# Two routed expert layers behind an attention: one stream of weight loads, and other places for rows, tables, scatters and steps

## The chip, the cores and the metric

One core of a Trainium2 chip runs the whole kernel. Its engines each work through their own list of instructions in a fixed order: TensorE (PE, matrix products and transposes), VectorE (DVE), ScalarE (ACT), GpSimd (POOL) and SyncE (SP, which here issues transfers); 16 DMA engines move the data. An instruction that has to wait holds up everything behind it on its engine. The metric is the time of one execution on the chip in microseconds (us), lower is better.

## The reference

Three stages follow each other. The first is an attention without softmax: for 8 batches and 8 heads, scores of 576 x 64 queries and keys, multiplied by a decaying causal mask, times the values. Its output is laid out as x, 4608 tokens of 512 columns.

The second is a mixture of experts (8 experts, 512 to 1024 to 512) in which each token goes to the one expert with the largest logit, weighted by its softmax value:

```python
logits = x @ w_gate
expert_idx = np.argmax(logits, axis=1)
...
for e in range(E):
    mask = expert_idx == e
    h = np.maximum(x[mask] @ w1[e], 0.0)
    out[mask] = gate_w[mask, None] * (h @ w2[e])
```

The third has the same shapes, but gives each expert exactly 576 tokens. All 4608 x 8 logits are gone through from the largest down, and a pair is taken if its token is free and its expert has room:

```python
for idx in np.argsort(-flat):
    tok, e = int(idx) // E, int(idx) % E
    if assigned[tok] >= 0 or counts[e] >= cap:
        continue
    assigned[tok] = e
    counts[e] += 1
```

and then each expert computes `np.maximum(x[mask] @ w1[e], 0.0) @ w2[e]` for its tokens.

## The kernel before, in words

Every matrix product is made of three products of halves: each float32 operand is split into a high and a low fp16 part, so that hi x hi, hi x lo and lo x hi give nearly float32. Weights arrive as float32 parts of 512 KB, eight per expert (four of w1, four of w2), in tiles named stage. ACT makes the high part (L384, w1h or w2h) and DVE the low part (L387, w1l or w2l). In `load_half` a half expert's loader issues three loads at once, converts a part at each of four later steps, and issues its fourth load after its first conversion. The next half's loads begin when its own loader is begun.

The order of work is written by hand around PE. `layer1` (L499) gives back control after every matrix product, `layer2` (L525; half tiles L521) too, and at numbered steps other work is put between them. Layer 1 of an expert has 192 such steps over its 640 rows, layer 2 has five tiles of 24. What is marked by `pe(...)` keeps its place in the written order; the rest is moved by the scheduler.

The first mixture (`moe1`): for each expert a list of its tokens is made (`cover` L537 to L539 on DVE, products L560 on PE, index arithmetic L563 to L569 on DVE), five gathers of 128 rows are issued on POOL (L418), and each row tile is squared and summed (L428 on DVE or L430 on ACT), scaled (L311 to L313, L443, L446, L447; POOL copies two columns, L448) and turned into columns (transposes on PE, or by DMA, L457). P0 holds the steps for expert 0's own list and its last two row tiles, N0, N1 and N6 those for the next expert's rows while experts 0, 1 to 5, and 6 run. L505 is the DVE operation that makes the low half of the hidden layer and so frees PE's result buffer. Tables for tokens beyond an expert's 640 rows (`overflow_tables`, DVE from L691 and one product, L769) are done a piece at a time in steps 38, 45, 52, ... of experts 2 and 3. Rows to fill gaps are scattered on POOL (L859) at steps of expert 6.

Layer 2 of experts 6 and 7 is put off: it runs while the second mixture makes its first choice.

The second mixture (`moe2`) runs eight phases. In each, `choose` finds the next expert and its tokens while an expert is computed: a threshold search (key L1268, comparisons L1272, counts on PE L1278 and L1287), the sums (L1310), the expert's number (es, L1318, read by SP, which then can load its weights), the table (V, L1334 or L1341; base L1345, copied at L1350), and the list (L537 to L539, L560). PACE and FIRST say how many PE columns go by between the steps, and GAP how many between tasks such as a conversion. The result rows are scattered to the output on POOL (L1446).

Of the kernel before, what the change touches and what calls it, by code (L numbers as in the profile page):

```python
# [9 lines left out]
F32 = mybir.dt.float32  # L10
# [17 lines left out]
SOON = 3  # L28
P0 = (3, 8, 52, 60)
N0 = (56, 76, 110, 130, 150, 170, 190)  # L30
N1 = (2, 32, 82, 102, 122, 142, 170)
# [310 lines left out]

def load_half(k, o, w, n, dve=0, spare=False, steps=True, behind=False):


    tc, nc = k.tc, k.nc
    if n == 1:
        o.wp = k.wp2 if k.wn % 2 else k.wp
        k.wn += 1
        o.w1h = o.wp.tile([128, 4, 1024], F16, name="w1h")  # L350
        o.w1l = o.wp.tile([128, 4, 1024], F16, name="w1l")
        h, l, shape, v = o.w1h, o.w1l, [128, 4, 256], w.rearrange("(c p) f -> p c f", p=128)
        at = lambda x, i: x[:, :, i * 256:(i + 1) * 256]
    else:
        if spare:
            o.w2h, o.w2l = (k.wp2.tile([128, 4, 1024], F16, name=x).rearrange("p c (a f) -> p (c a) f", a=2) for x in ("w1h", "w1l"))
        else:
            o.w2h = o.wp.tile([128, 8, 512], F16, name="w2h")
            o.w2l = o.wp.tile([128, 8, 512], F16, name="w2l")
        h, l, shape, v = o.w2h, o.w2l, [128, 2, 512], w.rearrange("(c p) f -> p c f", p=128)  # L360
        at = lambda x, i: x[:, 2 * i:2 * i + 2, :]

    def load(i):
        t = k.wp.tile(shape, F32, name="stage", bufs=3)
        d = nc.sync.dma_start(t, at(v, i))
        if behind:
            tc.keep_in_program_order(d)
        stages.append(t)

    stages = []  # L370
    for i in range(3):
        load(i)
    for i in range(4):
        yield
        t = stages[i]
        if i >= dve:
            if steps:
                pe(k, nc.scalar.activation(at(h, i), t, AF.Copy, scale=128.0))
            else:
                nc.scalar.activation(at(h, i), t, AF.Copy, scale=128.0)  # L380
            pe(k, nc.gpsimd.tensor_scalar(t, t, 128.0, 1.0, op0=OP.mult, op1=OP.mult))
            nc.gpsimd.tensor_tensor(at(l, i), t, at(h, i), op=OP.subtract)
        else:
            d = nc.scalar.activation(at(h, i), t, AF.Copy, scale=128.0)  # L384
            if steps:
                pe(k, d)
            d = nc.vector.scalar_tensor_tensor(at(l, i), t, 128.0, at(h, i), op0=OP.mult, op1=OP.subtract)  # L387
            if steps:
                pe(k, d)
        if i == 0:  # L390
            load(3)
    if n == 2:
        o.whole = True


def load_w(k, w1, w2, dve=0, spare=False):

    o = K()
    run(load_half(k, o, w1, 1, dve, steps=False))
    run(load_half(k, o, w2, 2, dve, spare, False))  # L400
    return o
# [21 lines left out]
def scale2(k, x, sc, q, dve=False, pin=False):  # L423

    nc = k.nc
    if dve:
        q = k.fp.tile([128, 512], mybir.dt.bfloat16, name="sq", bufs=1)
        nc.vector.scalar_tensor_tensor(q, x, 1.0, x, op0=OP.mult, op1=OP.mult, accum_out=sc[:, 0:1])  # L428
    else:
        d = nc.scalar.activation(q.bitcast(mybir.dt.bfloat16), x, AF.Square, accum_out=sc[:, 0:1])  # L430
        if pin:
            pe(k, d)
    normalizer(nc, sc[:, 0:1], sc[:, 1:2], sc[:, 2:3])


def normalise(k, xg, dve=False, to=None, pin=False):


    nc = k.nc
    h, sc = to or (k.fp.tile([128, 1024], F16, name="xhl", bufs=2), k.fp.tile([128, 6], F32, name="sc", bufs=12))  # L440
# [7 lines left out]
    nc.gpsimd.tensor_copy(sc[:, 4:6], xg[:, 512:514])  # L448
    return h, sc
# [152 lines left out]
def gate2(k, w, n):  # L602

    nc = k.nc
    pg = k.fps.tile([128, 8, 16], F32, name="tp")
    for i in range(4):
        t = k.fp.tile([128, 2, 8, 128], F16, name="w2T", bufs=2)
        for z, x in enumerate((w.w2h, w.w2l)):
            nc.sync.dma_start(t[:, z], x[:, 2 * i:2 * i + 2, :].rearrange("p f d -> p (f d)"), transpose=True)
# [41 lines left out]

def early(k, X, w1):


    nc = k.nc
    first = load_half(k, k.w[0], w1, 1, 2)
    next(first)
    yield
    yield
    for _ in range(4):  # L660
        next(first, None)
        yield
# [145 lines left out]
def moe1(k, X, X1, w1, w2):  # L808
# [6 lines left out]
    def prep(e):  # L815
# [47 lines left out]
    k.pin = True  # L863
    side = overflow_tables(k)
    x1, g, hs, ws, gates = None, {}, {}, {}, {}
    for e in range(8):
        w = ws[e] = k.w[e]
        steps = {}
        if e < 6:
            k.w[e + 1] = o = K()  # L870
            parts = [load_half(k, o, w1[e + 1], 1, 4), load_half(k, o, w2[e + 1], 2, 4)]
            if e == 0:
                parts[:0] = [load_half(k, w, w2[0], 2, 4)]
            if e == 5:
                k.w[7] = o = K()
                parts.append(load_half(k, o, w1[7], 1, 4))
        else:
            parts = [load_half(k, k.w[7], w2[7], 2, 4)] if e == 6 else []
        loader = chain(*parts)

        def load():
            next(loader, None)

        if e:
            load()
        for i in range(4, 190, 20) if e == 0 else range(13, 190, 30) if e == 5 else (16, 64, 112, 160):
            steps[i] = load
# [8 lines left out]
        if x1:  # L896
# [17 lines left out]
        if e == 6:  # L914
            for j in range(10 - LATE):
                steps[124 + 10 * j] = partial(put, k.fill, j, last)
        if e == 7:
# [15 lines left out]
        if e < 6:  # L933
            x1 = columns(e)
            for s in range(5):
                last = second(e, s, mixed(layer2(k, hs[e], w, s), {8: load, 18: load if e in (0, 5) and s < 2 else (lambda: None)}), x1)
    run(side)
# [512 lines left out]
def moe2(k, X1, w1, w2, out, rest):  # L1450
# [8 lines left out]
    def choices():  # L1459

        for ph in range(8):
            for t in choose(k, ph, lambda es: ev.setdefault(ph, nc.sync.value_load(es[0:1, 0:1], min_val=0, max_val=7)),
                            lambda ix: lx.setdefault(ph, ix)):
                yield (PACE if ph else FIRST)[t]

# [6 lines left out]

    def half(n, i):

        w = weights.setdefault(n, K())
        g = load_half(k, w, (None, w1, w2)[i][ds(ev[n], 1)].rearrange("o d f -> (o d) f"), i, 4)
        tasks.extend([(i == 1, lambda: next(g, None))] * 5)

# [21 lines left out]
    def prepare():  # L1500

        n = state.ph + 1
        if n == 0:
            if 0 in ev and 0 not in weights:
                half(0, 1)
        elif n in lx and n not in weights:
            half(n, 1)
            t = tasks[-5:]
            del tasks[-5:]
# [59 lines left out]
    turns[:] = [partial(turned, 0, s) for s in range(SOON, 5)]  # L1569
    half(0, 2)  # L1570
    for ph in range(8):
# [15 lines left out]
def program(tc, q, kk, v, wg1, w11, w12, wg2, w21, w22, consts, out, dbg=None):  # L1587
# [11 lines left out]
    select_setup(k)  # L1599
    k.w = {0: K()}  # L1600
    attention(k, q, kk, v, g1, X, early(k, X, w11[0]))
    open_ffn(k)
# [37 lines left out]
```

## Time and profile before

| | |
|---|---|
| median of 3 runs | 1130.11 us (1129.94 to 1133.36) |
| the profiled execution | 1129.93 us |
| its span, first to last instruction | 1128.1 us |
| mean granted TensorE clock | 0.978 |
| PE busy | 1061.4 us, 94% of the span |
| DVE busy | 668.7 us, 59% |
| ACT busy | 481.4 us, 43% |
| attention | 0 to 222 us |
| first mixture | 222 to 629 us; layer 2 of experts 6 and 7 until 697 us |
| second mixture | 697 to 1118 us; last scatter to 1128.1 us |

How to read the rows below: in a timeline a row has its start and its length in us, the engine, the line in the source, the operation with output<-input and shapes, and in brackets how long the engine had been idle before it and what released it. In a table of windows a row has the stretch in us, its length, the busy time and count of PE, its weight loads (PEld), DVE, ACT and POOL, then the granted clock of PE (1.00 is 2.4 GHz, 0.50 is 1.2 GHz), the share of the DMA engines and their GB/s. A row of waits has the waiting instruction, what it waited for, the sum over the run, how often, and the longest.

### The profile page before, as it was taken

To read this page: it belongs to the slowest core of one execution; us is meant where nothing else is said; L and a number is where in the kernel's file an instruction comes from. 1 tells how busy PE (TensorE), PEld (TensorE's weight loads), DVE (VectorE), ACT (ScalarE), POOL (GpSimd) and SP (SyncE) were. 2 spreads that over 40 slices of the span, in tenths; PEclk is the share of its full clock that TensorE was granted. 3 is DMA by queue.
4 is the path that set the end of the run, shared out by engine and by line. 5 is a ranking of instruction groups with operands and counts; after the bars stand their busy time and mean duration, and the time that the engine had idled before them with its cause. 6 is when DMAs were issued, how large, how long until landed. Compare 5 with 4: busy or idle time off the path is not lost. (4 is left out here: it accounts for less than half of the span.)

```text
span 1128.1 us, 25795 instructions
## 1 busy us (share of the span) xinstructions
PE 1061.4 (94%) x10279; PEld 682.9 (61%) x10279; DVE 668.7 (59%) x1662; ACT 481.4 (43%) x851; POOL 340.7 (30%) x589
## 2 busy tenths in 40 slices
PE   7999999789998999999989989899999999999996
PEld 5778877555646464746457534656565656567573
DVE  5787888775648455647553476747566646634140
ACT  5777766455545354536442124322233222224231
POOL 5766775041202020212040023323324141431101
PEclk9999999799999999999989999899999999999998
DMA  9999882349767677777966025538367392784211
GB/s 239 225 252 233 204 219 74 114 160 220 179 171 169 142 192 171 178 178 196 253 143 104 11 94 149 161 102 189 110 184 182 104 214 91 175 205 142 88 62 44
DMA packets 307520, 178.32 MB, mean 158 GB/s; under 512 B 241408, under 2 KB 274176, under 8 KB 307392
## 3 DMA queue, kind: packets, MB, share of 16 engines
q1 hardware_dynamic: 296928, 144.24, 52.6%
q0 software_dynamic: 10464, 32.34, 9.3%
q8 instruction: 84, 1.38, 0.5%
q14 instruction: 44, 0.36, 0.1%
HBM read 116.82 MB, written 31.28 MB: 131 GB/s over the span
## 5 line engine op out<-in xcount | busy, mean ns | idle before, releaser
L499 PE MATMUL ph<-xT,w1h 128*128 128x320 f16 (+4 forms) x2048 | 374.3, 299 | 11.9 <-DVE sc L312 4.9
L499 PEld LDWEIGHTS <-w1h 128*128 128x128 f16 x2048 | 200.3, 100 | 89.9 <-issue 24.3
L499 PE MATMUL ph<-xT,w1l 128*128 128x320 f16 (+4 forms) x1024 | 233.8, 299 | 0.0
L525 PE MATMUL py<-w2h,hh 128*128 128x512 f16 x536 | 203.2, 379 | 2.8 <-DVE key L1268 2.2
L525 PE MATMUL py<-w2l,hh 128*128 128x512 f16 x536 | 203.3, 379 | 0.0
L525 PE MATMUL py<-w2h,hl 128*128 128x512 f16 x536 | 203.2, 379 | 0.0
L525 PEld LDWEIGHTS <-hh 128*128 128x128 f16 x1072 | 103.1, 98 | 120.1 <-issue 4.9
L504 ACT ACTIVATE hh<-ph 128x576 f16<-128x576 f32 (+4 forms) x136 | 83.3, 613 | 181.7 <-PE ph L499 177.4
L505 DVE SCALAR_TENSOR_TENSOR hl<-ph,hh 128x576 f16<-128x576 f32 (+4 forms) x136 | 97.8, 719 | 69.0 <-ACT hh L504 67.9
L499 PEld LDWEIGHTS <-w1l 128*128 128x128 f16 x1024 | 100.9, 100 | 35.6 <-issue 3.3
L387 DVE SCALAR_TENSOR_TENSOR w1l<-stage,w1h 128x1024 f16<-128x1024 f32 x62 | 75.6, 1222 | 59.2 <-ACT w1h L384 58.1
L525 PEld LDWEIGHTS <-hl 128*128 128x128 f16 x536 | 52.4, 98 | 60.3
L387 DVE SCALAR_TENSOR_TENSOR w2l<-stage,w2h 128x1024 f16<-128x1024 f32 x64 | 78.3, 1224 | 12.0 <-ACT w2h L384 10.9
L384 ACT ACTIVATE w2h<-stage 128x1024 f16<-128x1024 f32 x64 | 66.9, 1048 | 8.7 <-DMA stage<-in_moe_w_dram 8.5
L430 ACT ACTIVATE x1r<-py 128x512 bf16<-128x512 f32 x40 | 23.8, 596 | 108.9 <-PE py L525 64.9
L384 ACT ACTIVATE w1h<-stage 128x1024 f16<-128x1024 f32 x62 | 64.2, 1046 | 8.7 <-DMA stage<-in_moe_w_dram 8.7
L1446 POOL DMA_INDIRECT out_dram<-x1r,ti x20 | 21.0, 1051 | 127.5 <-ACT x1r L1445 105.7
L1446 POOL DMA_INDIRECT out_dram<-w2T,ti x20 | 22.4, 1122 | 122.7 <-ACT w2T L1445 104.4
L418 POOL DMA_INDIRECT xg<-X1s,ix x40 | 44.7, 1116 | 44.2 <-DVE zf L1372 24.3
L583 POOL COPY x1r<-sc 128x1 f32<-128x1 f32 x37 | 8.5, 232 | 158.8 <-DMA X1s<-x1r 93.0
L187 DVE TENSOR_TENSOR sh<-pS,ct 128x1024 f16<-128x1024 f32 x36 | 43.9, 1220 | 17.3 <-PE pS L184 17.2
L147 POOL TENSOR_TENSOR vl<-vf,vh 128x512 f16<-128x512 f32 x36 | 41.7, 1159 | 36.1 <-ACT vh L146 28.9
(370 smaller groups left out, 1780.1 us busy)
## 6 DMA issues: line engine op xcount, KB each, us to landing
stage<-in_moe_w_dram SPq DMA_DIRECT2D x128, 512.0 KB, 4.1
Xs<-xr SPq DMA_DIRECT2D x36, 257.0 KB, 4.4
X1s<-x1r SPq DMA_DIRECT2D x33, 257.0 KB, 3.2
k<-in_k_dram SPq DMA_DIRECT2D x32, 256.0 KB, 4.3
q<-in_q_dram SPq DMA_DIRECT2D x32, 256.0 KB, 4.1
v<-in_v_dram SPq DMA_DIRECT2D x32, 256.0 KB, 4.4
k<-in_k_dram SPq DMA_DIRECT2D x8, 128.0 KB, 3.5
q<-in_q_dram SPq DMA_DIRECT2D x8, 128.0 KB, 3.7
```

What stands on the lines that cost most here:

```text
L147: nc.gpsimd.tensor_tensor(d.vl, d.vf, d.vh, op=OP.subtract)
L187: nc.vector.tensor_tensor(f(d.sh), f(pS), both, op=OP.mult)
L384: d = nc.scalar.activation(at(h, i), t, AF.Copy, scale=128.0)
L387: d = nc.vector.scalar_tensor_tensor(at(l, i), t, 128.0, at(h, i), op0=OP.mult, op1=OP.subtract)
L418: nc.gpsimd.indirect_dma_start(out=xg[:M], out_offset=None, in_=src, in_offset=bass.IndirectOffsetOnAxis(ap=gidx[:M], axis=0))
L430: d = nc.scalar.activation(q.bitcast(mybir.dt.bfloat16), x, AF.Square, accum_out=sc[:, 0:1])
L499: pe(k, nc.tensor.matmul(ph[:, z, :b], x[:, c, F], xT[:, y + c, a:a + b], start=i == 0, stop=i == 11))
L504: nc.scalar.activation(oh, src, AF.Relu)
L505: nc.vector.scalar_tensor_tensor(ol, src, 0.0, oh, op0=OP.max, op1=OP.subtract)
L525: pe(k, nc.tensor.matmul(py, x[:, f, S], y[:, f, :], start=i == 0, stop=i == 23))
L583: nc.gpsimd.tensor_copy(xr[:, 513:514], sc[:, 5:6])
L1446: nc.gpsimd.indirect_dma_start(out=out2 if tail else out, out_offset=bass.IndirectOffsetOnAxis(ap=ti, axis=0), in_=y, in_offset=None)
```

## The change

It has these parts, and what they compute is the same.

- `load_parts` takes the place of `load_half`. One stream holds all 64 parts of the first mixture; three loads are issued at the start, and after each conversion the load three parts on, over the borders of halves and experts. A number of parts that may be converted by the end of each expert caps it: (12, 20, 28, 36, 44, 56, 60, 60). In the second mixture each phase has such a stream over its w1 and w2.
- Expert 0's last two row tiles are normalised apart, at steps 40 and 60, and turned at 66 and 86 (before: normalised together, turned at 52 and 60); the next expert's rows come at 34, 70, 126, 146 and 168 and two in layer 2; xhl has three buffers instead of two. Conversions in expert 0 are 24 steps apart instead of 20.
- The overflow tables go through experts 1 to 4 at every 14th step instead of 2 and 3 at every 7th.
- The fill scatters are issued after the row tiles' last POOL copy (`issue_after`).
- In the first choice the list of PE's columns changes (base 3400 instead of 2000, list 1900 instead of 900), the key of phase 1 comes 5600 behind, and GAP is 3000 instead of 3800. Tasks stand in another order. The transposes of `gate2` keep their place on SP.
- The last phase computes its half tile first and a full tile last.

```diff
-P0 = (3, 8, 52, 60)
-N0 = (56, 76, 110, 130, 150, 170, 190)
+P0 = (3, 8, 40, 60, 66, 86)
+N0 = (34, 70, 126, 146, 168)
...
-FIRST = dict(key=2600, cnt=1700, any=1200, dig=800, sum=1900, base=2000, list=900)
-GAP = 3800
+FIRST = dict(key=2600, cnt=1700, any=1200, dig=800, sum=1900, base=3400, list=1900)
+AFTER_FIRST = 5600
+GAP = 3000
...
-def load_half(k, o, w, n, dve=0, spare=False, steps=True, behind=False):
...
-    for i in range(3):
-        load(i)
-    for i in range(4):
-        yield
...
-        if i == 0:
-            load(3)
+def load_parts(k, halves, steps=True):
...
+    for i in range(3):
+        load()
+    for m, ((o, w, n, dve, spare), i) in enumerate(parts):
+        yield
...
+        d = [nc.scalar.activation(h, t, AF.Copy, scale=128.0)]
...
+            d.append(nc.vector.scalar_tensor_tensor(l, t, 128.0, h, op0=OP.mult, op1=OP.subtract))
...
+        load()
...
-            normal = [normalise(k, x, True) for x in rows[e]]
+            normal = []
+            for x in rows[e]:
+                yield
+                normal.append(normalise(k, x, True, pin=True))
...
+    def fill(j, xr):
+        with k.tc.issue_after(k.copied.ins):
+            put(k.fill, j, xr)
...
+        due = (12, 20, 28, 36, 44, 56, 60, 60)[e]
         def load():
-            next(loader, None)
+            if k.parts < due:
+                k.parts += 1
+                next(k.loader, None)
...
-        if e in (2, 3):
-            for i in range(38, 192, 7):
+        if e in (1, 2, 3, 4):
+            for i in range(38, 192, 14):
...
-            tasks.extend([(True, partial(fetched, n))] + t[:2] + r[:2] + t[2:3] + r[2:4] + t[3:4] + r[4:] + t[4:])
-            half(n, 2)
+            tasks.extend(t[:1] + [(True, partial(fetched, n))] + t[1:3] + r[:2] + t[3:4] + r[2:4] + t[4:5] + r[4:] + t[5:])
...
-        for s in range(5):
+        for s in range(5) if ph < 7 else (4, 0, 1, 2, 3):
```

In expert 6 POOL's list had the scatters of fill rows (L859) around the gathers (L418) and the copies (L448) of expert 7's rows:

```order
L582 TENSOR_TENSOR x1r<-nm,sc 128x1
L850 COPY x1s<-x1r 128x1
L859 DMA X1s<-x1r,fill_7416 4736x514
L418 DMA xg<-Xs,ix 128x514 x5
L859 DMA X1s<-x1r,fill_7416 4736x514
L448 COPY sc<-xg 128x2 x4
L859 DMA X1s<-x1r,fill_7416 4736x514 x2
L448 COPY sc<-xg 128x2
L859 DMA X1s<-x1r,fill_7416 4736x514 x3
```

Now, with the lines of the changed source (L418 is L416 there, L859 is L861):

```order
L852 COPY x1s<-x1r 128x1
L582 TENSOR_TENSOR x1r<-nm,sc 128x1
L852 COPY x1s<-x1r 128x1
L416 DMA xg<-Xs,ix 128x514 x5
L448 COPY sc<-xg 128x2 x5
L861 DMA X1s<-x1r,fill_7281 4736x514 x7
```

All five gathers and all five copies now stand ahead of the seven scatters.

DVE's list at the first choice's lists, before. Two covers (L537 to L539, for two tables V) follow each other, then the index arithmetic:

```order
L1362 TENSOR_SCALAR few<-few 128x1
L537 TENSOR_SCALAR G<-iota_73,be 128x640
L538 TENSOR_SCALAR nV<-V_11162 128x44
L539 TENSOR_SCALAR G<-iota_73,be 128x640
L537 TENSOR_SCALAR G<-iota_73,be 128x640
L538 TENSOR_SCALAR nV<-V 128x44
L539 TENSOR_SCALAR G<-iota_73,be 128x640
L563 TENSOR_TENSOR lw<-slot_77,tp 128x5
```

The same place now (L312 to L314 are L311 to L313 of before, L1366 is L1362):

```order
L1366 TENSOR_SCALAR few<-few 128x1
L537 TENSOR_SCALAR G<-iota_73,be 128x640
L538 TENSOR_SCALAR nV<-V_11162 128x44
L539 TENSOR_SCALAR G<-iota_73,be 128x640
L387 SCALAR_TENSOR_TENSOR w1l<-stage,w1h 128x4x256
L312 TENSOR_SCALAR nm<-nm 128x1
L313 TENSOR_SCALAR nm<-nm 128x1
L314 TENSOR_SCALAR nm<-nm 128x1
L581 SCALAR_TENSOR_TENSOR x1r<-py,nm,x1r 128x512
L537 TENSOR_SCALAR G<-iota_73,be 128x640
L538 TENSOR_SCALAR nV<-V 128x44
L539 TENSOR_SCALAR G<-iota_73,be 128x640
```

A conversion of the phase's first part and the writing of a result row (L312 to L581) stand between the two covers. On PE the distance from the sums (L1310) to the base (L1345) goes from 10 products of L525 to 16, and from the base to the lists (L560) from 5 to 9.

DVE's list between the base and the second choice's lists (phase 1), before:

```order
L1350 COPY be<-tp 128x1
L1351 TENSOR_TENSOR be<-be,V 128x1
L1352 CAST V<-be 128x1
L505 SCALAR_TENSOR_TENSOR hl<-ph,hh 128x384
L387 SCALAR_TENSOR_TENSOR w2l<-stage,w2h 128x1024
L537 TENSOR_SCALAR G<-iota_73,be 128x640
L538 TENSOR_SCALAR nV<-V 128x44
L539 TENSOR_SCALAR G<-iota_73,be 128x640
```

and now (L1354 is L1350):

```order
L1354 COPY be<-tp 128x1
L1355 TENSOR_TENSOR be<-be,V 128x1
L1356 CAST V<-be 128x1
L505 SCALAR_TENSOR_TENSOR hl<-ph,hh 128x192
L537 TENSOR_SCALAR G<-iota_73,be 128x640
L538 TENSOR_SCALAR nV<-V 128x44
L539 TENSOR_SCALAR G<-iota_73,be 128x640
```

The conversion has left this place, and the hidden-layer operation ahead of the cover has half as many columns, since the choice now meets the second part of layer 1.

## Rows read from the trace of the kernel before

**Rows 1.** Page, engines' busy time; groups, last column idle before and releaser.

```profile
PE 1061.4 (94%) x10279; PEld 682.9 (61%) x10279; DVE 668.7 (59%) x1662; ACT 481.4 (43%) x851; POOL 340.7 (30%) x589
...
L384 ACT ACTIVATE w2h<-stage 128x1024 f16<-128x1024 f32 x64 | 66.9, 1048 | 8.7 <-DMA stage<-in_moe_w_dram 8.5
```

**Rows 2.** Waits of PE over the run: total us, times, longest us.

```profile
PE tp L560 <- DVE G L537: 5.6, 5, 2.8
PE tp L1345 <- DVE V L1334: 5.2, 4, 2.3
PE ph L499 <- DVE sc L312: 4.9, 2, 3.8
...
PE tp L1287 <- DVE r L1283: 2.9, 2, 2.1
...
PE tp L1278 <- DVE cmp L1272: 1.7, 1, 1.7
...
PE tp L1345 <- DVE V L1341: 1.1, 1, 1.1
```

**Rows 3.** Windows, layer 1 of experts 0, 1, 2, 6 with 7.

```profile
221.60:261.05 39.45, 33.09 (x225) 21.68 (x225) 28.59 (x89) 20.44 (x38) 13.70 (x23) 0.88 0.58 183
286.80:314.30 27.50, 27.50 (x244) 20.08 (x243) 20.35 (x55) 16.65 (x30) 7.13 (x14) 1.00 0.74 187
340.00:373.90 33.90, 30.56 (x245) 21.32 (x244) 27.12 (x98) 16.41 (x29) 8.27 (x14) 0.90 0.69 158
561.40:629.05 67.65, 62.55 (x647) 45.44 (x646) 30.34 (x87) 21.82 (x37) 13.58 (x19) 0.95 0.55 109
```

**Rows 4.** Windows, same columns, three stretches just after a wait of PE.

```profile
255.00:258.40 3.40, 3.39 (x19) 2.19 (x17) 2.69 (x7) 1.93 (x4) 0.17 (x2) 0.51 1.10 312
638.00:645.00 7.00, 6.60 (x39) 2.85 (x40) 3.78 (x12) 1.24 (x3) 1.19 (x2) 1.00 0.11 40
719.30:726.10 6.80, 6.44 (x48) 5.91 (x49) 5.06 (x21) 0.94 (x3) 2.29 (x2) 0.50 0.37 109
```

**Rows 5.** Timeline, DVE and ACT, expert 0's layer 1: start, us, instruction.

```profile
233.86 0.69 DVE L428 SCALAR_TENSOR_TENSOR sq<-xg 128x512 bf16<-128x512 f32 x1 [2.00 <-DMA xg<-Xs,ix]
...
248.73 0.63 ACT L430 ACTIVATE xhl<-xg 128x512 bf16<-128x512 f32 x1 [1.76 <-DMA xg<-Xs,ix]
```

**Rows 6.** Timeline of DVE, POOL and ACT, layer 1 of expert 6.

```profile
567.84 0.17 DVE L569 TENSOR_SCALAR ix<-lw 128x5 int32<-128x5 f32 x1
...
569.73 1.06 POOL L859 DMA_INDIRECT X1s<-x1r,fill  x1 [6.28 <-DMA X1s<-x1r]
571.09 0.98 POOL L418 DMA_INDIRECT xg<-Xs,ix  x1 [0.31 <-DVE hl L505]
...
574.48 0.63 ACT L430 ACTIVATE xhl<-xg 128x512 bf16<-128x512 f32 x1 [4.44 <-DMA xg<-Xs,ix]
```

**Rows 7.** Timeline of PE, SP, DVE and ACT around the first choose's lists.

```profile
663.26 0.17 PE L1310 MATMUL tp<-s,one_h 128*128 128x8 f16 x1
...
665.45 1.59 SPq L365 DMA_DIRECT2D stage<-in_moe_w_dram  x3
...
663.71 0.69 ACT L580 ACTIVATE x1r<-py,nm 128x512 f16<-128x512 f32 x1 [0.50 <-DVE frem L1314]
...
664.48 0.75 DVE L581 SCALAR_TENSOR_TENSOR x1r<-py,nm,x1r 128x512 f16<-128x512 f32 x1
...
668.32 0.38 DVE L537 TENSOR_SCALAR G<-iota,be 128x640 f16<-128x640 f16 x1
...
668.76 0.19 PE L560 MATMUL tp<-V,G 128*128 128x44 f16 x1 [0.76 <-DVE G L537]
...
669.14 1.06 ACT L384 ACTIVATE w1h<-stage 128x1024 f16<-128x1024 f32 x1 [4.75 <-DMA stage<-in_moe_w_dram]
```

**Rows 8.** Timeline of DVE before the second choose's lists.

```profile
717.92 1.23 DVE L387 SCALAR_TENSOR_TENSOR w2l<-stage,w2h 128x1024 f16<-128x1024 f32 x1 [0.39 <-ACT w2h L384]
```

**Rows 9.** Timeline of POOL, the last scatter to the output.

```profile
1120.09 0.96 POOL L1446 DMA_INDIRECT out_dram<-w2T,ti  x1 [2.55 <-DMA out_dram<-x1r,ti]
```

More of the change, by code (lines that the diff above doesn't have):

```diff
@@ L340, in moe_setup, with load @@
     k.wn = k.xn = 0
-def load_half(k, o, w, n, dve=0, spare=False, steps=True, behind=False):
[L346 to L355, printed above, removed]
+def load_parts(k, halves, steps=True):
+    nc = k.nc
+    parts = [(h, i) for h in halves for i in range(4)]
+    stages = []
+    def load():
+        if len(stages) < len(parts):
+            (o, w, n, *_), i = parts[len(stages)]
+            w = w() if callable(w) else w
+            t = k.wp.tile([128, 4, 256] if n == 1 else [128, 2, 512], F32, name="stage", bufs=3)
+            v = w.rearrange("(c p) f -> p c f", p=128)
+            nc.sync.dma_start(t, v[:, :, i * 256:(i + 1) * 256] if n == 1 else v[:, 2 * i:2 * i + 2, :])
+            stages.append(t)
+    for i in range(3):
+        load()
+    for m, ((o, w, n, dve, spare), i) in enumerate(parts):
+        yield
+        if i == 0 and n == 1:
+            o.wp = k.wp2 if k.wn % 2 else k.wp
+            k.wn += 1
+            o.w1h = o.wp.tile([128, 4, 1024], F16, name="w1h")
+            o.w1l = o.wp.tile([128, 4, 1024], F16, name="w1l")
+        elif i == 0 and spare:
@@ L356, in load_half @@
             o.w2h, o.w2l = (k.wp2.tile([128, 4, 1024], F16, name=x).rearrange("p c (a f) -> p (c a) f", a=2) for x in ("w1h", "w1l"))
-        else:
+        elif i == 0:
             o.w2h = o.wp.tile([128, 8, 512], F16, name="w2h")
             o.w2l = o.wp.tile([128, 8, 512], F16, name="w2l")
[L360 to L368, printed above, removed]
@@ L370, in load_half @@
-    stages = []
-    for i in range(3):
-        load(i)
-    for i in range(4):
-        yield
-        t = stages[i]
+        h, l = ((x[:, :, i * 256:(i + 1) * 256] for x in (o.w1h, o.w1l)) if n == 1 else
+                (x[:, 2 * i:2 * i + 2, :] for x in (o.w2h, o.w2l)))
+        t = stages[m]
+        d = [nc.scalar.activation(h, t, AF.Copy, scale=128.0)]
+        if steps:
+            pe(k, d[0])
         if i >= dve:
+            d.append(nc.gpsimd.tensor_scalar(t, t, 128.0, 1.0, op0=OP.mult, op1=OP.mult))
@@ L649, in moe1_tables, with early @@
     nc.vector.tensor_copy(k.cnt, pb[:, 1, :])
-def early(k, X, w1):
+def early(k, X):
     nc = k.nc
-    first = load_half(k, k.w[0], w1, 1, 2)
-    next(first)
+    next(k.loader)
     yield
@@ L660, in early @@
     for _ in range(4):
-        next(first, None)
+        next(k.loader)
         yield
@@ L868, in moe1 @@
         steps = {}
[L869 to L879, printed above, removed]
+        due = (12, 20, 28, 36, 44, 56, 60, 60)[e]
         def load():
-            next(loader, None)
+            if k.parts < due:
+                k.parts += 1
+                next(k.loader, None)
         if e:
             load()
-        for i in range(4, 190, 20) if e == 0 else range(13, 190, 30) if e == 5 else (16, 64, 112, 160):
+        for i in range(4, 190, 24) if e == 0 else range(13, 190, 30) if e == 5 else (16, 64, 112, 160):
             steps[i] = load
@@ L915, in moe1 @@
             for j in range(10 - LATE):
-                steps[124 + 10 * j] = partial(put, k.fill, j, last)
+                steps[124 + 10 * j] = partial(fill, j, last)
         if e == 7:
@@ L935, in moe1 @@
             for s in range(5):
-                last = second(e, s, mixed(layer2(k, hs[e], w, s), {8: load, 18: load if e in (0, 5) and s < 2 else (lambda: None)}), x1)
+                at = {8: load}
+                if e in (0, 5) and s < 2:
+                    at[18] = load
+                if e == 0 and s == 0:
+                    at[2] = at[14] = lambda: next(p1, None)
+                last = second(e, s, mixed(layer2(k, hs[e], w, s), at), x1)
     run(side)
@@ L1463, in choices @@
                             lambda ix: lx.setdefault(ph, ix)):
-                yield (PACE if ph else FIRST)[t]
+                yield AFTER_FIRST if ph == 1 and t == "key" else (PACE if ph else FIRST)[t]
     choice = choices()
@@ L1471, in choose_on, with loads @@
         prepare()
-    def half(n, i):
+    def loads(n):
         w = weights.setdefault(n, K())
-        g = load_half(k, w, (None, w1, w2)[i][ds(ev[n], 1)].rearrange("o d f -> (o d) f"), i, 4)
-        tasks.extend([(i == 1, lambda: next(g, None))] * 5)
+        g = load_parts(k, [(w, (w1, w2)[i][ds(ev[n], 1)].rearrange("o d f -> (o d) f"), i + 1, 4, False) for i in range(2)])
+        return [(i < 5, lambda: next(g, None)) for i in range(9)]
     def soon():
```

46 lines of the change are left out of this document (21 added, 25 removed).

## The prediction, made before the changed kernel ran

> **What bounds the kernel now.** I read the page first: PE is busy 1061.4 of 1128.1 us, so some 67 us are idle, and about 25 us more go to a mean clock of 0.978 (0.022 of 1128.1) [rows 1]. The change takes no product away, so it can only win idle time and clock. ACT waited for weights (stage) 8.5 us in 64 conversions of w2 [rows 1], so loading ahead is worth little by itself. Next I read what PE waits for [rows 2]: nearly always a DVE operation of a list, a table or a row's scale (L537, L1334, L312, L1283), hardly ever the weights themselves. DVE is only 59% busy [rows 1], so what counts is what stands ahead of those operations in its list. Then I read the windows of layer 1, experts 0, 1, 2 and 6 with 7: the same work that takes expert 1 27.50 us with no idle PE takes expert 0 39.45 us (33.09 busy) and expert 2 33.90 (30.56 busy); experts 6 and 7 take 67.65 with 62.55 busy [rows 3]. The reader is to see that the loss is in few places, and that each place has two parts: the wait, and a slow clock behind it.
>
> **The clock.** After the wait for the second choice's lists (2.75 us long) the granted clock was 0.50, that is 1.2 instead of 2.4 GHz, for 6.80 us; in expert 0 it was 0.51 for 3.40 us; after a wait of 2.2 us for key (L1268, before 638) it stayed 1.00 [rows 4]. So in these rows a wait of 2.2 us costs itself, one of 2.8 or more another 3.4 us (half of 6.80); in expert 0, after several waits close together, 1.7 (half of 3.40). The same 3.4 is in the windows: 33.90 x 0.10 in expert 2, 67.65 x 0.05 in experts 6 and 7 [rows 3].
>
> **The sum, against the profiled execution of 1129.93 us** (span 1128.1 and 1.8 around it; 0.2 below the median of 1130.11, which I neglect). Within 0.3%, some 3.4 us, a measurement of this kernel can't tell from no change.
>
> *Expert 0.* 39.45 - 33.09 = 6.4 us are idle [rows 3]. DVE squares a gathered row in its fixed list and waits 2.00 us for it to land, and a tile of expert 1's rows lets ACT wait 1.76 us in the same manner; the hidden-layer operation that frees PE's buffers is queued behind [rows 5]. The change normalises expert 0's two rows apart and brings expert 1's rows at steps spread to 168 and into layer 2. Of the 6.4, 5.6 are these waits; they go, with the 1.7 of clock behind them. Against that, the low part of a w2 conversion (1.23 us, [rows 8]) now stands ahead of expert 0's list on DVE, and the first transpose on PE at step 66 waits for a row whose gather starts so much later: I put back one wait of 2.1 us and 1.7 of clock, since the chain from landing to transposes holds the same operations as before. That is -7.3 + 3.8 = -3.5. Ends: -7 (no new wait) and 0 (the waits only move).
>
> *Expert 2.* The table product (L769) waits 33.90 - 30.56 = 3.3 us for its DVE work; DVE is busy 27.12 of the 33.90 us [rows 3]. With every 14th step over experts 1 to 4 the pieces stand half as dense. Expert 1's 20.35 us of DVE [rows 3] gets half of what expert 2 has more (6.8 / 2 = 3.4) and one more conversion (1.2): some 25 of 27.5 us. That fits, so 3.3 and 3.4 of clock go: -6.7. Ends: -6.7 and -1, if DVE, 91% busy, lets PE wait once per expert.
>
> *Experts 6 and 7.* The list of expert 7's rows was ready at 568.0, but a scatter of fill rows was first on POOL, so the first gather went out at 571.09 and ACT had the row at 574.48, after 4.44 idle us [rows 6]; PE then waited 3.8 us for that row's scales (L312) [rows 2] and ran 6.8 us at half clock, by the window's 0.95 [rows 3]. With scatters last, gathers go out 3 us earlier. PE's longest wait is gone or under 1 us, and the clock stays: -3.8 - 3.4, and 0.7 of a wait for a row's transpose near 597, which is late for the same reason: -7.9. Ends: -8 and -3 (a part of the wait stays, without the clock drop, as at 638). The seven scatters, now behind the copies, have from about 578 to 629, where the first mixture ends, and nothing reads their rows sooner.
>
> Expert 5 gets seven conversions instead of five in layer 1, and two fewer in layer 2: 0 ± 1. First mixture: -3.5 - 6.7 - 7.9 = -18.1.
>
> *First choice.* The base waited 1.1 us (V L1341), a comparison 1.7 (L1278) [rows 2], the lists 0.76 [rows 7]; more products now lie ahead of each: -3.6. But between the two covers on DVE now stand the low part of w1's first part, three small operations and a result row's writing. By the rows: the sums on PE are at 663.26; the parts are issued at 665.45, and ACT begins w1h at 669.14, when the part has landed, having waited 4.75 us [rows 7]. The change leaves that chain as it is, since the expert's number comes from the sums. Then w1h ends at 670.2, w1l at 671.4, the small operations at 671.7, ACT's 0.69 at 672.4, L581's 0.75 at 673.2, the first L537 of the second cover (0.38) at 673.5 [rows 7, 8]. PE reaches the lists 16 and 9 products of 512 columns after the sums; at 27.50 us for expert 1's 192 products of 320 columns [rows 3], 0.23 us each, that is 5.7 us later, at 669.0. So the list's product, which took 0.76 us of waiting, now **waits 4.5 us**: more than the 2.75 that was followed by half clock, so 3.4 more. Sum: -3.6 + 4.5 + 3.4 = +4.3. Ends: -3.6 and +8.
>
> What the Trainium skill states bears on this ("TensorE: Matmul & The Clock Gate", section "HAM oscillation — how this bites in real kernels"): an idle PE is throttled again and then runs cold, and the extra time is half of the time throttled. The trace agrees (rows 4: 6.80 us at 0.50 behind 2.75 us); by it the wait is paid nearly twice, and without it the sum would be 3.4 us lower.
>
> *Second choice (phase 0).* The lists waited 2.75 us behind a conversion of 1.23 us [rows 2, 8], the base 0.7 us, and 3.4 of clock followed [rows 4]. The conversion has left that place and the hidden-layer operation ahead is half as long. About 1.1 us of waiting stays: -5.7. Ends: -6.9 and -2.
>
> *Later phases.* In phase 1 a conversion still stands ahead of the base (wait of 2.3, [rows 2]) and a second now ahead of the lists: +1.2. The waits for L1283, up to 2.1 us [rows 2], came from a part that landed late; the part is now three ahead: -2.1 - 0.8, and 0.7 of a list wait. So -2.4, ends -5 and +6.
>
> *End.* The last full tile's scatter waits for none like the half tile's, which stood 2.55 us behind the one before [rows 9], but moves twice the bytes: -0.5, ends -2 and +1.
>
> **Sum:** -18.1 + 4.3 - 5.7 - 2.4 - 0.5 = -22.4, so 1107.5, rounded to **1108 us**.
>
> **The rivals.**
> 1. *No wait at the first choice's lists.* If the part lands earlier (SP issues it sooner, or PE is later there than I count), the 4.5 + 3.4 fall away: 1108 - 8 = 1100. For it: only ACT's wait for the landing makes the delay. Against: the issue hangs on the sums, and 5.9 us from the sums to the landing are in the rows [rows 7]. Chance 0.13.
> 2. *DVE fuller than I count.* With 25 of 27.5 us in layer 1 of experts 1 to 4, each hidden-layer operation may come late; expert 0's waits only move (0 instead of -3.5), expert 2's gain is half lost (+3.4) and experts 6 and 7 keep a part (+3): 1118. For it: 27.12 us in expert 2 made PE wait [rows 3]. Against: expert 1's PE was never idle. Chance 0.22. The skill has a rule of the same direction for loads ("DMA: Bandwidth & Descriptors", section "Issuing engines are not separate DMA queues"): all transfers interleave on the same 16 engines, so more loads in flight only share them; by it the gathers, not the weights, would come later. No row here shows a gather slowed by a load, and the DMA share in these windows was 0.55 to 0.74 [rows 3].
> 3. *Slower.* One in-order stream puts a conversion that waits for its part ahead of the lists not only in the first choice but in the phases as well: 4.5 + 3.4 = 7.9 each. With three such phases it has eaten the 22 us; with four, 1108 + 32 = 1140. For it: two places in the changed order (the first choice, phase 1) have it. Against: in phases the parts are issued long before, three ahead. Chance 0.06.
> 4. *Nothing gained.* PE's waits move to the next instruction of the same DVE list, so that only experts 6 and 7 gain and the first choice gives it back: 1129. Chance 0.06.
>
> **How the numbers follow.** Forecast 0.53 (1104 to 1113), rival 1 0.13, rival 2 0.22, rivals 3 and 4 0.06 each. The range from 1098 to 1122 holds the forecast, nearly all of rivals 1 and 2, and leaves out 3 and 4. Faster by over 0.3% (under 1126.7): forecast, rivals 1 and 2, 0.88. Slower (over 1133.5): 0.05, part of rival 3. Same: 0.07.
>
> **What would show it.** Right: expert 2's layer 1 near 27.5 us at clock 1.00; experts 6 and 7 near 60 us, with POOL's first gather within 0.5 us after the list; the product L560 of the first choice waiting over 4 us with a conversion (L387) just before on DVE, and half clock behind it; phase 0's list wait under 1 us. Wrong: an idle PE in layer 1 of expert 1, 3 or 4 (rival 2), no wait at the first lists (rival 1), or waits over 2.7 us at lists of several phases (rival 3).

## The result, and the profile after

The changed kernel is **slower**: median 1143.16 us (1141.2 to 1145.04, 4 runs), before 1130.03 (1127.82 to 1133.36, 4 runs), ratio 1.0114 with a 95% interval from 1.0090 to 1.0138. The forecast was 1108. The profiled execution of the changed kernel took 1144.38 us with a span of 1142.6.

The page of the changed kernel, its span and the busy time of each engine, which answers to [rows 1]:

```profile
span 1142.6 us, 25769 instructions
...
PE 1058.9 (93%) x10279; PEld 677.5 (59%) x10279; DVE 670.5 (59%) x1662; ACT 481.3 (42%) x851; POOL 332.9 (29%) x589
```

The work is the same, PE is only idle longer: 84 us instead of 67. What PE waits for in the changed kernel (total us, times, longest us), which answers to [rows 2]:

```profile
PE tp L560 <- DVE G L537: 10.4, 7, 4.4
...
PE tp L1282 <- DVE cmp L1276: 6.9, 4, 3.1
PE tp L1349 <- DVE V L1338: 6.3, 3, 4.8
PE tp L1291 <- DVE r L1287: 4.7, 4, 3.1
PE ph L499 <- DVE hl L505: 4.6, 5, 1.8
PE tp L614 <- DMA w2T<-w2h: 4.2, 1, 4.2
...
PE ph L499 <- DVE sc L313: 1.5, 2, 0.9
...
PE tp L615 <- DMA w2T<-w2l: 1.1, 1, 1.1
```

The wait of the overflow tables' product (3.3 us) is gone, and the waits for rows' scales have shrunk (sc L313 is L312 of before, 4.9 us there). Others have grown in their place: lists from 5.6 to 10.4, comparisons from 1.7 to 6.9, r from 2.9 to 4.7 (L1291 is L1287 of before), the hidden layer's low half (hl) from 0.8 to 4.6. The waits for tables V add up to 6.3 in both kernels, but the longest went from 2.3 to 4.8. One wait is new: the transposes of `gate2` (w2T). Where the stretches begin and end (first product of each to the next) tells where the time went:

| stretch, us | before | changed | forecast of the difference |
|---|---|---|---|
| until expert 0's layer 1 | 221.6 | 223.9 | 0 |
| expert 0, layer 1 | 39.3 | 37.1 | -3.5 |
| expert 2, layer 1 | 33.8 | 28.6 | -6.7 |
| experts 1, 3, 4, 5, layer 1 together | 110.6 | 115.0 | 0 |
| experts 6 and 7, layer 1 | 67.5 | 69.7 | -7.9 |
| their layer 2, with the first choice | 68.4 | 71.4 | +4.3 |
| phases 0 to 4 and layer 1 of phase 5 | 303.1 | 314.3 | -8.1 |
| last product to the end | 9.95 | 9.4 | -0.5 |

Layer 2 of expert 5, which is not in the table, is 0.8 us shorter; layer 2 of experts 0 to 4 takes 25.9 us in both. The attention's own instructions are the same in both; most of its 2.3 us come from a load of v that landed late (PE waited 1.5 us for POOL's vf near 62 us), and in the later profiles expert 0 began anywhere from 219 to 222. Layer 1 of experts 0, 1, 2, and 6 with 7 in the changed kernel, the windows that answer to [rows 3]:

```profile
223.88:260.97 37.09, 31.76 (x224) 20.92 (x224) 29.37 (x90) 20.15 (x37) 12.59 (x23) 0.91 0.61 173
286.87:315.57 28.70, 27.83 (x244) 20.10 (x243) 24.19 (x74) 16.62 (x29) 6.31 (x14) 1.00 0.72 189
341.47:370.05 28.58, 27.85 (x245) 20.10 (x243) 23.71 (x76) 17.57 (x30) 8.15 (x14) 1.00 0.79 194
559.93:629.62 69.69, 61.46 (x646) 44.81 (x645) 30.58 (x87) 22.15 (x37) 12.99 (x19) 0.95 0.61 120
```

Expert 2 keeps its clock (1.00) as forecast and takes 28.6 us, where the forecast's gain would have left 27.1. Expert 1, which had no idle PE, now has 0.9 us and reads 28.70. Experts 6 and 7 still have 8.2 us idle and a clock of 0.95: of these, 1.8 are a wait for expert 7's cover, 0.9 for a row's scales and 5.3 for w2T, which take the place of the wait that went. Three places show how the time was lost.

**Expert 6.** Timeline of POOL, ACT, SP and PE in the changed kernel, which answers to [rows 6]:

```profile
568.13 0.98 POOL L416 DMA_INDIRECT xg<-Xs,ix  x1 [6.19 <-DVE ix L569]
...
571.53 0.63 ACT L430 ACTIVATE xhl<-xg 128x512 bf16<-128x512 f32 x1 [1.63 <-DMA xg<-Xs,ix]
...
574.31 5.69 SPq L457 DMA_TRANSPOSE xT<-xhl  x2
580.05 1.32 SPq L609 DMA_TRANSPOSE w2T<-w2h  x1
...
583.01 0.20 PE L614 MATMUL tp<-wg2s,w2T 128*128 128x16 f16 x1 [4.20 <-DMA w2T<-w2h]
```

The gather is 3 us earlier and the row's square too, as forecast. But SP holds the w2T transposes, pinned to their written place, behind two row transposes (xT), of which the second waits for its row; PE comes 4 us sooner to the products that need w2T (578.8, before 582.8). Before the change the scheduler had issued the first w2T pair at 530.5.

**First choice.** Timeline of ACT, DVE and PE, which answers to [rows 7]: the wait of 4.5 us that was forecast is there, 4.38, for the reason given.

```profile
669.41 1.06 ACT L378 ACTIVATE w1h<-stage 128x1024 f16<-128x1024 f32 x1 [4.37 <-DMA stage<-in_moe_w_dram]
...
670.50 1.23 DVE L387 SCALAR_TENSOR_TENSOR w1l<-stage,w1h 128x1024 f16<-128x1024 f32 x1 [1.38 <-ACT w1h L378]
...
673.95 0.22 PE L560 MATMUL tp<-V,G 128*128 128x44 f16 x1 [4.38 <-DVE G L537]
```

**Seventh choice (phase 5's layer 1, 28.9 to 35.8 us).** Timeline of SP, ACT, DVE and PE:

```profile
972.09 3.08 SPq L457 DMA_TRANSPOSE xT<-xg  x2
975.43 0.88 SPq L358 DMA_DIRECT2D stage<-in_moe_w_dram  x1
...
982.83 1.06 ACT L378 ACTIVATE w2h<-stage 128x1024 f16<-128x1024 f32 x1 [4.23 <-DMA stage<-in_moe_w_dram]
...
983.92 1.23 DVE L387 SCALAR_TENSOR_TENSOR w2l<-stage,w2h 128x1024 f16<-128x1024 f32 x1 [4.06 <-ACT w2h L378]
985.06 0.15 DVE L1318 TENSOR_TENSOR frem<-frem,tp 128x8 f32<-128x8 f32 x1
...
987.25 0.18 PE L1349 MATMUL tp<-V,lt_h 128*128 128x1 f16 x1 [4.77 <-DVE V L1338]
```

Here the load of the part that ACT needs is issued at 975.43, behind two transposes of gathered rows. It lands at 982.81, 7.4 us after its issue (the median of these loads in the kernel before was 4.1): until 977.7 the packets that move for SP's transfers are those of the two transposes (2048 of 256 bytes), and only then come the 256 packets of 2 KB of the load. So the part comes late, ACT waits 4.23 us, DVE's conversion waits for ACT, and the choice's own small operations (frem, then V) stand behind that conversion. PE waits 4.77 us, and the clock is 0.50 for 10.3 us:

```profile
986.70:997.00 10.30, 7.63 (x41) 4.66 (x42) 5.47 (x20) 1.97 (x3) 1.72 (x2) 0.50 0.73 219
```

### The profile page after: what moved, and what is told of

Its sections match the earlier page's. It is cut to its first block, busy times and chain, and to the rows that moved or that the text cites. A ratio compares the mean times of both kernels' runs of the same rounds, so it can differ in the third digit from the quotient of the medians.

```text
span 1142.6 us, 25769 instructions
## 1 busy us (share of the span) xinstructions
PE 1058.9 (93%) x10279; PEld 677.5 (59%) x10279; DVE 670.5 (59%) x1662; ACT 481.3 (42%) x851; POOL 332.9 (29%) x589
## 5 line engine op out<-in xcount | busy, mean ns | idle before, releaser
L499 PE MATMUL ph<-xT,w1h 128*128 128x320 f16 (+4 forms) x2048 | 367.1, 296 | 7.3 <-DVE hl L505 4.6
L499 PEld LDWEIGHTS <-w1h 128*128 128x128 f16 x2048 | 197.4, 99 | 78.0 <-issue 14.5
L499 PE MATMUL ph<-xT,w1l 128*128 128x320 f16 (+4 forms) x1024 | 230.7, 296 | 0.0
L525 PE MATMUL py<-w2h,hh 128*128 128x512 f16 x536 | 203.3, 379 | 2.2 <-DVE key L1272 2.2
L525 PE MATMUL py<-w2l,hh 128*128 128x512 f16 x536 | 203.3, 379 | 0.0
L525 PE MATMUL py<-w2h,hl 128*128 128x512 f16 x536 | 203.2, 379 | 0.0
L525 PEld LDWEIGHTS <-hh 128*128 128x128 f16 x1072 | 103.1, 98 | 119.1 <-issue 3.7
L499 PEld LDWEIGHTS <-w1l 128*128 128x128 f16 x1024 | 99.8, 99 | 36.9 <-issue 5.5
L525 PEld LDWEIGHTS <-hl 128*128 128x128 f16 x536 | 52.4, 98 | 60.4 <-issue 0.6
L416 POOL DMA_INDIRECT xg<-X1s,ix x40 | 45.0, 1125 | 46.2 <-DVE zf L1376 26.5
L1450 POOL DMA_INDIRECT out_dram<-w2T,ti x20 | 19.7, 987 | 127.5 <-ACT w2T L1449 90.4
L416 POOL DMA_INDIRECT xg<-Xs,ix x37 | 40.2, 1087 | 52.3 <-DVE ix L569 38.0
```

What stands on the lines that cost most here:

```text
L416: nc.gpsimd.indirect_dma_start(out=xg[:M], out_offset=None, in_=src, in_offset=bass.IndirectOffsetOnAxis(ap=gidx[:M], axis=0))
L499: pe(k, nc.tensor.matmul(ph[:, z, :b], x[:, c, F], xT[:, y + c, a:a + b], start=i == 0, stop=i == 11))
L525: pe(k, nc.tensor.matmul(py, x[:, f, S], y[:, f, :], start=i == 0, stop=i == 23))
L1450: nc.gpsimd.indirect_dma_start(out=out2 if tail else out, out_offset=bass.IndirectOffsetOnAxis(ap=ti, axis=0), in_=y, in_offset=None)
```

## The experiments

Theory A: the loss comes from orders on SP and DVE, namely parts late behind transposes with tasks 3.0 us apart in the second mixture, and the pinned transposes in the first. (FIRST, PACE and GAP count PE columns divided by 2.4, not columns: 3000 is 3.0 us at the full clock.) Each run below has its own runs of the kernel before on the same chip; those medians were 1130.8 (first four), 1131.4 (transposes_after_w1 and the three from gap_and_unpinned on), 1124.4 (the four of best) and 1125.2 (the two edits of the kernel before), so across groups ratios are compared, not times. The changed kernel ran in a group of its own (1130.03), so a difference from its 1143.16 is good to some 3 us: for the same edit the ratio gives up to 3 us more.

### Which half, and which edit

**moe1_new_moe2_old** and **moe1_old_moe2_new** swap the second mixture's function with its loader, and FIRST and GAP. **gate2_unpinned** and **gap_3800** undo one edit each:

```diff
-            pe(k, nc.sync.dma_start(t[:, z], x[:, 2 * i:2 * i + 2, :].rearrange("p f d -> p (f d)"), transpose=True))
+            nc.sync.dma_start(t[:, z], x[:, 2 * i:2 * i + 2, :].rearrange("p f d -> p (f d)"), transpose=True)
```
```diff
-GAP = 3000
+GAP = 3800
```

> The changed first mixture with the second mixture of before (its loader, its FIRST and GAP, its task order, its tile order). In the changed kernel the stretch from the start of phase 0 to the end of the last product took 432 us, before 421. Theory A (the loss sits in the second mixture, where conversions wait for parts that stand behind transposes on SP): those 11 us come back, and the 7.8 us of the first choice's lists too, since FIRST is the old one and its tasks also; the first mixture's 9 us of the gate2 transposes stay: 1143 - 11 - 5 = about 1127. Rival B (the loss sits in the first mixture and the delays of the second only follow from where it begins): about 1140.

Measured 1137.38, ratio 1.0047 (1.0022 to 1.0072): with the changed first mixture alone the kernel loses 6.6 us, where A expected it to be faster than before (1127), so A missed by 10 us. Its profile does not place the loss in the first mixture: from the start to the end of layer 1 of experts 6 and 7 it is 1.7 us shorter than the kernel before (expert 2 5.2 shorter, experts 6 and 7 3.3 longer with a wait of 4.3 us for w2T). The loss stands behind that, in code that was not changed: 2.5 us in layer 2 of experts 6 and 7, 3.6 in layer 1 of phase 0 and 6.5 in layer 1 of phase 2. What lengthens those has not been shown.

> The first mixture of before with the changed second mixture. Theory A: 1130 + 11 (phases) + 5 (first choice's lists) = about 1144, with ACT waiting near 17 us for parts after 700 us as in the changed kernel. Rival B: near 1130.

Measured 1142.49, ratio 1.0104 (1.0072 to 1.0136). With the changed second mixture alone the kernel loses 11.7 us. B, which had this run near 1130, falls as the whole account; that time can be lost behind the first mixture without a change there, as B says, the run before this one does show.

> The changed kernel, with gate2's transposes on SP free to be moved by the scheduler as before. Theory A: the wait of PE for w2T near 578 us (4.2 + 1.1 us) goes, since the first pair is issued some 40 us earlier, and the half clock of 6.8 us behind it too (3.4): 1143 - 8.7 = about 1134.5. Rival: PE then waits at the next row's scales or transposes in the same place, and only 2 us or less come back: 1141.

Measured 1135.01, ratio 1.0023 (0.9995 to 1.0051): 8.2 us come back (0.9% by the ratios). PE no longer waits for w2T, and experts 6 and 7 take 63.1 us at clock 1.00:

```profile
559.00:622.10 63.10, 59.87 (x650) 43.83 (x649) 30.64 (x85) 21.59 (x36) 13.75 (x19) 1.00 0.57 115
```

Layer 2 of expert 5 is 2.1 us longer in this profile than in the changed kernel's, with a wait of 1.9 us for a result row; that has not been taken apart.

> The changed kernel with GAP 3800 instead of 3000, the tasks of the second mixture as far apart as before, everything else as changed. Theory A: the conversions come later than their parts, ACT's waits for parts after 700 us fall from 17 us to under 9, and the long waits of the seventh choice (4.8 + 2.0 us and 5 of clock) go: 1143 - 8 = about 1135. Rival C (the stream's order, not the distance, does it: a load behind the transposes is late at any distance): 1141 to 1145.

Measured 1134.47, ratio 1.0011 (0.9988 to 1.0034): 8.7 us come back (1.0% by the ratios), so C, by which no distance would help, falls. ACT's waits for parts after 700 us (total us, times, longest us) in the changed kernel:

```profile
ACT w2h L378 <- DMA stage<-in_moe_w_dram: 17.0, 6, 5.9
```

and in gap_3800, where PE waits 0.6 us for the seventh choice's table (V) instead of 4.8, but 2.4 for its lists instead of 2.0:

```profile
ACT w2h L378 <- DMA stage<-in_moe_w_dram: 1.7, 2, 1.4
```

### Why the parts are late

**transposes_after_w1** keeps GAP 3000 and changes the place alone:

```diff
-            tasks.extend(t[:1] + [(True, partial(fetched, n))] + t[1:3] + r[:2] + t[3:4] + r[2:4] + t[4:5] + r[4:] + t[5:])
+            tasks.extend(t[:1] + [(True, partial(fetched, n))] + t[1:5] + r + t[5:])
```

> The changed kernel (GAP 3000), with the transposes of a phase's rows placed behind all four conversions of w1, so the loads of the next parts stand ahead of them on SP. If a load's place behind transposes that wait for gathered rows makes the parts late, ACT's waits for parts after 700 us fall from 17 us to under 9 and the seventh choice's waits (4.8 + 2.0) mostly go: about 1136. If the distance of 3.0 us between conversions is by itself too short for a 512 KB part, the waits stay: 1141 to 1146.

Measured 1136.22, ratio 1.0039 (1.0025 to 1.0054): about 7 us of the loss gone without more distance. ACT's waits after 700 us in this kernel are half:

```profile
ACT w2h L378 <- DMA stage<-in_moe_w_dram: 8.5, 3, 4.1
```

So the place behind the transposes makes parts late, and more distance (gap_3800) hides it. Of the seventh choice's waits only the table's went (0.6 us); its lists wait 3.5 us here, behind a wait of ACT of 4.1 us for a part, so that part of the expectation missed. The waits for comparisons belong to neither: they are 6.9 us in the changed kernel and 7.2 in gap_3800.

**before_gap_3000** puts the short distance into the kernel before.

> The kernel before, with GAP 3000 instead of 3800 alone. If the short distance between conversions is enough by itself to make parts late: ACT waits more than 8.5 us for parts after 700 us and the time is about 1136. If it takes the stream with it (each load issued behind the conversion before and the transposes), the old loader, which issues three loads at once at the start of a half, loses nothing: 1127 to 1132, perhaps less, since the orders of conversions and lists change too.

Measured 1122.79, ratio 0.9979 (0.9954 to 1.0004): no loss. The short distance costs only together with the changed second mixture (its stream and its order of tasks). ACT waits longer for parts here than in the kernel before, 11.4 us after 700 us instead of 8.5, and yet nothing is lost: behind its two longest waits, 3.7 and 3.9 us, PE waits 0.9 us at the most. So ACT's waiting is by itself no cost; what stands behind the conversion on DVE decides.

**before_pinned** puts the pin alone into the kernel before.

> The kernel before, with gate2's transposes pinned on SP alone. If the pin by itself makes PE wait for w2T in expert 6: SP's order puts the first pair behind expert 7's second row tile, which there is later still than in the changed kernel, so PE waits 5 us or more, with 3.4 of clock unless the clock is down already from the wait for the scales: 1134 to 1140. Rival (the wait for the scales, 3.8 us, that stands there covers it): 1130.

Measured 1131.58, ratio 1.0069 (1.0044 to 1.0093), so 6 to 8 us by itself. Layer 1 of experts 6 and 7 takes 74.2 us instead of 67.5. PE's waits in that kernel:

```profile
PE tp L614 <- DMA w2T<-w2h: 6.1, 1, 6.1
...
PE tp L615 <- DMA w2T<-w2l: 1.4, 1, 1.4
```

### What the rest is worth

**gap_and_unpinned** undoes both edits. **gap_unpinned_step6** also moves one conversion, **gap_unpinned_first_old** also restores the first choice's two numbers:

```diff
         if e:
-            load()
+            steps[6] = load
```
```diff
-FIRST = dict(key=2600, cnt=1700, any=1200, dig=800, sum=1900, base=3400, list=1900)
+FIRST = dict(key=2600, cnt=1700, any=1200, dig=800, sum=1900, base=2000, list=900)
```

> The changed kernel with both: GAP 3800, and gate2's transposes free. The two sit in different stages (expert 6's layer 1; phases 1 to 6), so their gains add: 1143 - 8.2 - 8.7 = about 1126, below the kernel before (1130.8). Rival: the scheduler's new order on SP gives a part back, 1130 or more.

Measured 1127.30, ratio 0.9958 (0.9941 to 0.9974): the two add, and the kernel before is beaten.

> As gap_and_unpinned, and the first conversion of experts 1 to 6 at step 6 of layer 1 instead of step 0, so behind the next expert's cover on DVE and not ahead of it. In the changed kernel layer 1 of experts 1 to 5 took about 1.2 us more than the undisturbed 27.3: 0.65 us wait for the cover (L537, L539), the rest waits named issue; expert 6 waited 1.8 us. If the conversion ahead of the cover is the cause: 0.65 x 4 + 1.8 = 4.4 us less than gap_and_unpinned, near 1122. Rival (DVE is simply fuller, with the tables in four experts): no difference beyond 1 us.

Measured 1122.16, ratio 0.9912 (0.9887 to 0.9937), 5.1 us less, so the conversion's place does cost. The profile bears out less than the expectation's account: layer 1 of experts 1 to 5 is 0.3 to 0.7 us shorter each, 2.4 together, and still 0.5 to 0.8 above 27.3 in experts 1 to 4. In layer 1 of expert 6 the wait for the cover falls from 1.8 to 0.4 us, but a wait of 1.9 for a row's scales comes in its place, and the stretch takes 63.7 us as against 63.3. Where the rest of the 5.1 comes from is not shown. In the changed kernel's expert 1, DVE does the conversion first and the cover after it:

```profile
289.94 1.22 DVE L387 SCALAR_TENSOR_TENSOR w1l<-stage,w1h 128x1024 f16<-128x1024 f32 x1
291.08 0.38 DVE L537 TENSOR_SCALAR G<-iota,base 128x640 f16<-128x640 f16 x1
```

> As gap_and_unpinned, with base 2000 and list 900 in FIRST, as before, so the first choice's lists come ahead of the conversion of the phase's first part (DVE's order shows the two covers together again). The wait of 4.4 us and 3.4 us of clock go; the old waits of 1.1, 0.8 and 1.7 come back: -7.8 + 3.6 = -4.2, near 1122. Rival: the second choice, which then lies earlier, gets a conversion ahead of its table (DVE's order has one) and gives back 3 us or more: 1125 to 1129.

Measured 1116.99, ratio 0.9865 (0.9839 to 0.9890), 10.3 us less than gap_and_unpinned, more than twice what was expected. The trace has 1.4 us of it in layer 2 of experts 6 and 7, 1.3 in layer 1 of phase 1 and 3.6 in that of phase 5 (30.25 to 26.61). The likely reason is that the numbers shift every later choice against its conversions, which was not priced; no run tests it.

**best** has both; the last three undo one part of the first mixture in it.

> gap_unpinned_first_old with the first conversion of experts 1 to 6 at step 6: the two sit in different stages, so the 5.1 us that step 6 gave come on top: 1117.0 - 5 = about 1112. Rival: part of the 5 us was paid in the first choice that is now cheaper, 1114 to 1116.

Measured 1112.29, ratio 0.9893 (0.9853 to 0.9933), on a chip that runs the kernel before in 1124.4. As a time it is what was expected; as a ratio it doesn't beat gap_unpinned_first_old, within the intervals. Expert 1, and experts 6 and 7, in best:

```profile
283.42:310.75 27.33, 27.33 (x243) 20.02 (x242) 24.34 (x75) 16.97 (x30) 7.09 (x14) 1.00 0.82 201
552.69:614.62 61.93, 59.66 (x647) 44.27 (x646) 30.07 (x87) 21.83 (x37) 13.54 (x20) 1.00 0.61 120
```

Expert 1 has no idle PE with 24.34 us of DVE work in 27.33, so a fuller DVE by itself costs nothing there.

```diff
-                steps[124 + 10 * j] = partial(fill, j, last)
+                steps[124 + 10 * j] = partial(put, k.fill, j, last)
```

> best, with the fill scatters put where they were (one ahead of expert 7's gathers on POOL, one between gathers and copies). If moving them is what saves the wait of 3.8 us and its 3.4 us of clock in expert 6: 1112 + 7 = about 1119. Rival (another wait in the same place would have taken its place, the scatters were not the cause): 1112 to 1114.

Measured 1112.74, ratio 0.9896 (0.9853 to 0.9939): no 7 us. In the profile the scatters do cost: experts 6 and 7 take 66.2 us at clock 0.97, not 61.9, but their layer 2 is 2.0 shorter, because there the clock did not fall. The timed runs cannot tell 4 us from nothing (both intervals reach over 4 us to either side), so only the 7 us are ruled out.

```diff
-        if e in (1, 2, 3, 4):
-            for i in range(38, 192, 14):
+        if e in (2, 3):
+            for i in range(38, 192, 7):
```

> best, with the overflow tables in experts 2 and 3 at every 7th step as before. Experts 1 to 4 together took 4 x 28 us in the changed form; with the old form expert 2 gets its wait of 3.3 us and 3.4 us of clock back, and experts 1 and 4 may lose up to 0.5 us each: 1112 + 6 = about 1118. Rival (the stream of loads, not the tables, freed expert 2): about 1112.

Measured 1112.52, ratio 0.9899 (0.9868 to 0.9930): no difference in the timed runs. The one profiled execution, at 1123.7 the slowest of the six, has expert 2 at 32.7 us; the other five lie between 1111.6 and 1113.4. The profiles do settle what shortened expert 2: its layer 1 takes 30.1 to 33.8 us in all five with the tables in experts 2 and 3, this one with the stream, and 27.4 to 28.8 in the eleven with the tables in four experts. So it was the tables and not the stream; that this makes the whole kernel faster, the timed runs do not show.

**best_first_rows_as_before** restores P0, N0 and the joint normalising of expert 0's two rows, and with them the place of the next expert's last two rows in layer 1:

> best, with expert 0's two last rows normalised together and the next expert's rows at the steps of before (P0, N0). The prediction had 3.5 us for this part, the changed kernel took 37.1 instead of 39.3 in expert 0, and 35.4 to 36.6 in later runs: 1112 + 3.5 = about 1115.5. Rival (the gain came from the conversions standing 24 steps apart): 1112.

Measured 1111.31, ratio 0.9881 (0.9831 to 0.9930). Expert 0 takes 35.15 us in it, 35.56 in best: this part gives nothing that shows; the rival stands, the conversions 24 steps apart or earlier loads did it (not told apart).

## Why the prediction was wrong, point by point

- **What bounds the kernel: right in part.** PE does wait for DVE's lists, tables and scales. But the two largest new costs begin in SP's list, with w2T and with parts that come late, and the prediction set the weights aside as worth little.
- **Expert 0 (-3.5): -2.2, between its ends (-7 and 0), wrong in cause.** The rows' places give nothing that shows (best_first_rows_as_before).
- **Expert 2 (-6.7): -5.2, right in mechanism.** Experts 1, 3, 4 and 5, taken at 0, cost 4.4 us together in layer 1 (3.6 with the 0.8 that expert 5 wins in layer 2). The failed step is "one more conversion (1.2)": it was counted as DVE time with 2.5 us to spare, and not by its place. The old loader's first step of an expert only issued loads; in the stream every step converts, so a conversion came to stand ahead of the cover. Moving it gave 0.3 to 0.7 us back in each expert (gap_unpinned_step6); for the rest of the 1.1 to 1.4 us that experts 1, 3 and 4 lost each the cause is open, since only best and its variants have these at 27.3, and best has the same first mixture as gap_unpinned_step6. Rival 2's condition, an idle PE in expert 1, came true, but not because DVE was full: in best it is as full with no idle PE.
- **Experts 6 and 7 (-7.9): +2.2.** The chain from scatter to row was right (gather 3 us earlier, the wait for scales 0.9 instead of 3.8). The failed step is the one that was left out: the pin of gate2's transposes stood in the change, and no term priced it. SP's list, in which it stands, was not read. Alone in the kernel before it costs 0.69%. Without it (gate2_unpinned) the stretch takes 63.1 us, 3.5 above the forecast; the wait for the cover (2.0) is the larger part of what is left.
- **First choice (+4.3): +3.0, right**, wait 4.38 for 4.5, half clock for 6.8 us behind it. What its numbers do to later choices was missed: the old ones gave back 10 us.
- **Second choice (-5.7) and later phases (-2.4): +11.2 together.** The wait of 2.75 us did go, and phase 0's layer 1 is 4.4 us shorter. The failed step is "the part is now three ahead": it is three ahead in the stream, but on SP loads stand behind transposes that wait for gathered rows, and with tasks 3.0 us apart conversions catch up with it. GAP was in the change and unpriced; it is worth 8.7 us. Layer 1 of phases 4 and 5, where late parts stand ahead of a choice, has 9.1 us of the loss. Phases 1 and 2 have 5.1 more; there PE waits 3.1 and 2.2 us for comparisons with no late part ahead of them, which no term had, and why it does is open. Rival 3 named this mechanism and its place, and was given 0.06; the reason given against it ("in phases the parts are issued long before") does not hold in SP's list.
- **The clock: half right.** Waits of 4.2 and 4.4 us went with 6.8 us of half clock as priced, the one of 4.8 with 10.2. The changed kernel's waits of 3.1 us (L1282 and L1291) had none, while the wait of 2.15 us for key, with none in both kernels, had 3.4 us of it in best and others. The step "2.2 costs itself, 2.8 or more another 3.4" had two rows behind it and is no rule; the kernel before had a row against it, half clock at a wait of 2.28 us (V L1334 at 763.16):

```profile
763.70:767.10 3.40, 3.40 (x26) 2.31 (x24) 2.28 (x13) 0.00 (x0) 0.02 (x1) 0.50 0.49 155
```

The table's differences from the forecast, 2.3 + 1.3 + 1.5 + 4.4 + 10.1 - 1.3 + 19.3, make 37.6 us; with the 0.8 of expert 5's layer 2 taken off that is, but for rounding, the 36.9 us from 1107.5 (the sum before rounding to 1108) to the profiled 1144.4.

## What to carry to other kernels

Running ahead is a property of a queue, not of a loop: a load issued three parts on was early here only where no transpose that waited stood before it on the engine that issues it, so read that engine's list and not only the one that computes. When a step changes from issuing to computing, or is pinned, price its new place against every consumer behind it. A small number that only sets distances (GAP, FIRST) moves all later work against each other and deserves a term of its own.

## What was not expected of the hardware

The kernel before ran at 1130.8 and 1131.4 in two groups of runs and at 1124.4 and 1125.2 in two others: 0.6%, as much as several of the edits are worth, so that only ratios within a group tell them apart. In the changed kernel the product groups L595 and L596 in layer 1 of experts 1 to 4 have one idle time of 0.3 to 0.6 us each that the trace puts down to no release ("issue"); the kernel before has none, nor has expert 1 in best; gap_unpinned_step6, with the conversion behind the cover, still has them (0.3 to 0.7 us). Its cause stays open.
